# A fused linear-attention and gated-MLP kernel: raw weights ahead of fetches at the turn of the halves, stores of key/value sums spread over rounds, first folded weights in slots of x

## The chip, the cores and the metric

The kernel runs on one core of a Trainium2 chip. The metric is the device time in microseconds (us) from start to end; lower is better. The engines are named as the profile names them: PE (TensorE, matmuls), DVE (VectorE), ACT (ScalarE), POOL (GpSimd) and SP (SyncE, which here issues all transfers). Each engine works through a list of its own in order, and waits where an instruction needs another engine's or a transfer's result.

## The reference

With x of 2048 x 1024, 32 heads of 32 and a hidden width of 3584, all in fp32:

```
xn  = layernorm(x)
q, k, v = split(xn @ wqkv)                       # per head
phi(a) = concat(softmax(a @ w_phi), softmax(-a @ w_phi))
kv  = phi(k)^T @ v ;  z = sum over tokens of phi(k)
s   = ((phi(q) @ kv) / (phi(q) @ z + 1e-6)) @ wo
g   = silu((silu(xn @ w1) * (xn @ w3)) @ w2)
out = x + s * g
```

## The kernel before

**Products.** Each fp32 operand is split into a rounded part and a rest (fp32r), by `split`: ScalarE casts (L91), VectorE subtracts (L92). A product is three passes over these. Blocks of 2 x 2 are multiplied with seven products in place of eight, in the order A11, A12, S2, S1, S3, S4, A22 (`ORDER`), with B-side operands B11, B21, T2, T1, T3, B22, T4; their sums are made by GpSimd (L126, L127, L270, L272) and, for x, by VectorE. TensorE accumulates the seven products in PSUM banks a, b and c.

**Prologue (0 to some 90 us).** x of the first token half is loaded, normalised, transposed and split into the seven operands for four quarters q. The weights of keys and queries are multiplied with w_phi once ("folded"): `first_folds` loads a block `wr`, multiplies it on TensorE (`fold`, L247, three PSUM buffers), lets ScalarE copy it back into `wr` (L311) and SP store it (L312). 22 blocks are folded here, the last nine in three groups of three between the splits of S3, S4 and A22. Their `wr` tiles come from tag "w" of the pool `work`, which has five slots and also holds T2 (`t`), the evicted gate and up results (`h`, `u`) and others. A slot of a fold is free again when its store has landed. The pool `xp` has 14 slots, for blocks of x, and is closed near the end of the first half.

**First stage (to some 1176 us).** Two token halves tb = 0, 1; 28 hidden tiles f each; seven products ("events") of twelve matmuls for each f. From step 7 on the order on all five engines is the program's own, written out by step tables, until the stage ends: `prep_at` says at which step an operand of B is split for (tb, f), normally four events ahead (`LEAD`), `load_at` when the raw weights two tiles on are loaded (`b_load`, L256, L257), one step after the last split of the present tile. Side work has steps of its own; in the second half it is the splitting of w2 and others (`side_w2`, loads `room<-in_w` at L516, sums on GpSimd, splits `w2o`). In the last tile of the first half (f = 27) each event from the first on is followed by the fetch of one operand of x of the second half, four transfers of 512 KB at L162, into the place of the operand just used. The second half begins with its tiles 0 to 6 interleaved in pairs: (0,0), (0,1), (1,0), (0,2), (1,1), and so on, written (f, product).

**Heads (to some 1507 us).** For each of two column halves c and eight pairs of token tiles i, `heads` computes keys and values in seven products, the feature map, and sums phi(k)^T v and z into one PSUM bank `pkv`. The operands of x for the next pair are loaded at the start of a pair (L565). When all pairs of c are summed, `kv_out` copies the sums into `kva` and `zs` and stores them with 16 small transfers (L737, L738), for c = 0 within pair 0 of c = 1, for c = 1 in round 1 of the next stage.

**w2 stage (to some 2040 us).** Rounds r over seven blocks kb and eight pairs of token tiles, with 42 matmuls each (`product`). `a_first` loads `hr` (L769, 512 KB) for the next round, subtracts (`sm`, L774) and splits; `a_second` makes the other operands (L782, L783). `product` evicts with ScalarE (L921) or adds on VectorE (L927); in later blocks ScalarE copies to `u` (tag "h1", two slots) and GpSimd adds. The order is the scheduler's here. Weights arrive by `load_b` (L762). Queries, attention and the output projection end the kernel.

Of the kernel before, what the change touches and what calls it, by code (L numbers as in the profile page):

```python
# [8 lines left out]
F = mybir.dt.float32  # L9
# [7 lines left out]
S, D, H, DH, FF = 2048, 1024, 32, 32, 3584  # L17
P = 128
NT = S // P
ND = D // P  # L20
NF = FF // P
# [7 lines left out]
def tile_kernel(ctx: ExitStack, tc: tile.TileContext, x, wkT, wqT, wv, wphi, wo, w1, w3, w2, out):  # L29
# [106 lines left out]
    work = pool("work", 5)  # L136
# [101 lines left out]
    def load_w(wT, dch, c, t=None):  # L238
        wr = blk("wr") if t is None else t
        nc.sync.dma_start(wr, wT[dch][:, 4 * c:4 * c + 4])  # L240
        return wr
# [37 lines left out]
    for t in range(8):  # L279
        if t in (4, 5):  # L280
            if t == 4:
                late = rwp.tile([P, 2, 2, 512], F, name="rw", tag="rw")
            r = late[:, t - 4]
        else:
            r = quad("xt", F).rearrange("p u k t -> p u (k t)")
        xs.append(load_x(t, [r[:, 0], r[:, 1]]))
        if t == 3:
            rws = [b_load(0)]
            early_w = [load_w(*folds[k][:3], work.tile([P, 4, P], F, name="wr", tag="w")) for k in range(4)]
# [3 lines left out]
    for j in range(4):  # L293
        sl = slice(32 * j, 32 * j + 32)
# [7 lines left out]

    at_fold = 0

    def first_folds(n):
        nonlocal at_fold
        for _ in range(n):
            wT, k, c, d = folds[at_fold]
            wr = early_w.pop(0) if early_w else load_w(wT, k, c, work.tile([P, 4, P], F, name="wr", tag="w"))
            pw = fold(wr, c)  # L310
            nc.scalar.copy(wr, pw)  # L311
            nc.sync.dma_start(d, flat(wr))  # L312
            at_fold += 1
# [42 lines left out]
    for n in ("S3", "S4", "A22"):  # L356
        next(b_gen)
        for q in range(4):
            first_split(n, q, raw[q][n])
        first_folds(3)  # L360


    def load_kv(c, k):
# [33 lines left out]
    for tb in range(2):  # L397
        for f in range(NF):
            own = [at_event[tb, f, j] for j in range(7)]
            steps = [k - LEAD for k in own]  # L400
            if (tb, f) == (1, 1):
                steps = [k - 2 for k in own]
            elif (tb, f) == (1, 2):
                steps = [own[0] + k for k in (-2, -2, -1, 0, 1, 2, 2)]
            if (tb, f) != (0, 0):
                for k in steps:
                    prep_at.setdefault(k, []).append((tb, f))
                sums_at.setdefault(steps[0] - (1 if tb and f in (1, 2) else 2), []).append((tb, f))
            late = divmod(NF * tb + f + 2, NF)
            if late[0] < 2:  # L410
                load_at.setdefault(max(steps[6] + 1, 0) if (tb, f) != (0, 0) else 0, []).append(late)
# [265 lines left out]
                nc.tensor.matmul(pkv[sl, m], e[:, m // 4, (m % 4) * P + 32 * h:(m % 4) * P + 32 * h + 32],  # L677
                                 v[:, 4 * (m % 4) + h], start=first and m == 0, stop=last, skip_group_check=True)

    pkv = None  # L680

    def heads(i, xo, wb, steps, pend):

        nonlocal pkv
        bank, first, last = {}, i == 0, i + 1 == len(pairs)
        for b, an, bn in ORDER:
            if b not in bank:
                bank[b] = ps.tile([P, 512], F, name=f"bank{b}", tag=f"bk{b}", bufs=BANKS[b])
            n = 0
            for k in range(4):  # L690
                for u, w in PASSES:
                    nc.tensor.matmul(bank[b], xo[an][:, u, k], wb[bn][:, w, k], start=an in ("A11", "A12", "S1") and n == 0,  # L692
                                     stop=LAST[b] == an and n == 11, skip_group_check=True)
                    n += 1
            pb, pv = bank[b], bank[b].rearrange("p (h d) -> p h d", d=DH)
            if an == "A11":
                k0 = work.tile([P, 512], F, name="k0", tag="w")
                nc.scalar.copy(k0, pb)
            elif an == "A12":
                nc.vector.tensor_add(k0, pb, k0)  # L700
                e0, v0 = room_ev()
                keys(k0, e0)
            elif an == "S2":
                d0 = value(v0)
                nc.scalar.copy(d0, pv)
            elif an == "S1":
                if pend:
                    kv(*pend)
                    if first:
                        kv_out(0, pkv)  # L710
                e1, v1 = room_ev()
                d1 = value(v1)
                nc.scalar.copy(d1, pv)
            elif an == "S3":
                nc.vector.tensor_add(d1, pv, d1)
            elif an == "S4":
                nc.vector.tensor_add(d0, pv, d0)
            else:
                if first:
                    pkv = ps.tile([P, 512], F, name="pkv", tag="kv", bufs=1)[:, :8 * (DH + 2)]  # L720
                    pkv = pkv.rearrange("p (h d) -> p h d", d=DH + 2)
                kv(pkv, first, False, e0, v0)
                keys(pb, e1)
            next(steps)
        return pkv, False, last, e1, v1

    def kv_out(c, pkv):
        kva = work.tile([P, 8, DH], F, name="kva", tag="w")
        zs = small.tile([P, 8], F, name="zs")
        nc.scalar.copy(kva, pkv[:, :, :DH])  # L730

        nc.vector.tensor_scalar_add(zs[:, :4], pkv[:, :4, DH], 1e-6)
        nc.vector.tensor_copy(zs[:, 4:], pkv[:, 4:, DH])
        for s in range(2):
            for j in range(4):
                sl = slice(32 * j, 32 * j + 32)
                nc.sync.dma_start(kv_d[j % 2, s, :, G * c + j // 2:G * c + G:2], kva[sl, 4 * s:4 * s + 4])  # L737
                nc.sync.dma_start(z_d[0, c, :, j, s].rearrange("g f -> f g"), zs[sl, 4 * s:4 * s + 4])  # L738

# [37 lines left out]
    def a_second(hq, sm, _):  # L779
        hr = hq.rearrange("p b (h k) t -> p b h k t", h=2)  # L780
        s34 = work.tile([P, 4, P], F, name="s34", tag="w")
        nc.vector.tensor_sub(s34[:, 0:2], hr[:, 1, 1], sm)  # L782
        nc.vector.tensor_sub(s34[:, 2:4], hr[:, 0, 1], sm)  # L783
        t1, t2 = quad("as"), quad("as")
        split(t1[:, 0], t1[:, 1], hq[:, 1])
        split(t2[:, 0], t2[:, 1], s34)
        return {"S1": (t1, 0), "A22": (t1, 2), "S3": (t2, 0), "S4": (t2, 2)}
# [146 lines left out]
    for r, new in enumerate(steps):  # L934
        kb, i = new or (NKB, 0)
        end = kb == NKB - 1
        if new is None:
            in_order(ENG.SP, ENG.Activation, ENG.DVE, ENG.Pool)
            xT = split_q(xf)
        if kb + 1 < NKB and 1 < i < 7:  # L940
            load_b(kb + 1, i - 2)
        parts = first
        if r + 1 < len(steps) - 1:
            first = a_first(*steps[r + 1])
        bank = {}
        for b, an, bn in TURN:
            if an in FIRST:
                if new:
                    product(kb, i, bank, r, parts[2], b, an, bn)
            elif old:  # L950
                product(*old, banks, r, second, b, an, bn)
                if new is None:
                    load_wo(2 * BNAMES.index(bn))
                    load_wo(2 * BNAMES.index(bn) + 1)
        if new:
            second = a_second(*parts) if r else ready[1]
        if r == 1:

            kv(*pend)
            kv_out(1, pkv)  # L960
            late_rw += [rwp.tile([P, 2, 2, 512], R, name="late", tag="rw") for _ in range(2)]
        if i + 1 == len(pairs):
            if end:
                for k in range(6):
                    load_wo(k)
            else:
                load_b(kb + 1, 5)
                load_b(kb + 1, 6)


        if end:
            if i:
                gate(*pairs[i - 1])
            if i in (1, 2):
                for k in range(4 * i - 4, 4 * i):
                    load_wq(1, k, ring("wq1"))
            if i == 3:
                zb = [flat(ring("zb").bitcast(F)) for _ in range(2)]
                for c in range(2):
                    nc.sync.dma_start(zb[c], z_d[:, c].rearrange("o g j s f -> o (g j s f)").to_broadcast([P, D]))  # L980
            if 1 < i < 6:
                for j, t in enumerate(pairs[i - 2]):
                    load_wq(0, 2 * i - 4 + j, accp.tile([P, 2, 512], R, name="wq0", tag=f"acc{t}"))
            if i == 4:
                xf = load_q(0)
            elif i == 5:
                xT = split_q(xf)
            elif i > 5:
                if i == 6:

                    kvu = work.tile([P, 2 * G, DH], F, name="kvu", tag="h1", bufs=2)
                    nc.sync.dma_start(kvu, kv_d.rearrange("a s f g d -> (a s f) g d"))
                es[7 - i] = queries(project_q(xT, 7 - i, "bka"), 7 - i)
            if i == 7:
                xf = load_q(1)
        old, banks = new, bank
# [94 lines left out]
```

## Time and profile before

| | |
|---|---|
| runs | 2465.31 us (median of 3; 2465.04 to 2466.66) |
| profiled execution | 2466.53 us, span 2464.8 us |
| TensorE busy | 2406.8 us, 98% of the span |
| mean granted TensorE clock | 0.996 |
| VectorE, ScalarE, GpSimd busy | 71%, 36%, 28% |
| transfers | 521 MB, mean 211 GB/s |

In a row of a timeline the first number is the start in us from the beginning of the span, the second the time of the row's instructions together, then engine, line, operation, what is written and read, the shapes and the count. Behind it, in brackets, stands the idle time of the engine ahead of the row and what ended it. In a list of waits stand the total, the number and the longest. A row of windows gives, for each engine in the order PE, weight loads, DVE, ACT, POOL, the busy time and count, then the granted clock, the share of the DMA engines and GB/s.

### The profile page before, as it was taken

Reading aid. Unit: us, or ns where it says so; the run is one execution under the profiler, and the core shown is the slowest. Engines: PE = TensorE matmul, PEld = TensorE weight load, DVE = VectorE, ACT = ScalarE, POOL = GpSimd, SP = SyncE. Lnnn points to the kernel's source line nnn. Section 1 sums busy time; section 2 is a strip of 40 time slices with the busy share of each in tenths; the row PEclk is TensorE's granted clock in tenths of the full one; section 3 lists DMA queues with packets and bytes.
Section 4 is the critical chain, followed back from the end, with each engine's and each line's share of the span. In section 5 each row is a group of like instructions: output and inputs, shape, how many; then the busy total and the mean of one; then the engine's idle time right before and its main releaser. Section 6 shows DMA issues by size and latency. Waiting matters only on the chain.

```text
span 2464.8 us, 35933 instructions
## 1 busy us (share of the span) xinstructions
PE 2406.8 (98%) x13648; PEld 1971.2 (80%) x13648; DVE 1748.6 (71%) x2573; ACT 887.4 (36%) x1555; POOL 681.8 (28%) x481
## 2 busy tenths in 40 slices
PE   5999999999999999999999999999999999999999
PEld 5788788888788888888788788788888887777877
DVE  8578876664688888764566565687878887777775
ACT  6455544443354454432111113422222244222221
POOL 2334554432455555431000000011111112232222
PEclk9999999999999999999999999999999999999999
DMA  8556999775988887755967763623444376223222
GB/s 296 170 198 228 328 320 303 260 230 175 303 296 293 288 296 278 247 179 199 354 211 297 271 204 123 235 95 138 179 171 180 109 280 232 93 73 92 76 86 69
DMA packets 300812, 521.02 MB, mean 211 GB/s; under 512 B 24544, under 2 KB 172000, under 8 KB 298848
## 3 DMA queue, kind: packets, MB, share of 16 engines
q1 hardware_dynamic: 300640, 518.74, 61.1%
q8 instruction: 107, 1.75, 0.3%
q14 instruction: 65, 0.53, 0.1%
HBM read 331.22 MB, written 187.44 MB: 210 GB/s over the span
## 4 chain that ended last, share of the span: by engine, by line
PE 84%; DVE 6%; DMA 4%; SPq 2%; issue 2%; ACT 1%; POOL 1%; ACTq 0%; DVEq 0%; POOLq 0%
PE bankb L598 19%; PE pm L100 14%; PE bankb L915 12%; PE bankc L598 9%; PE bankb L692 7%; PE bankc L915 6%; PE banka L598 5%; PE bankc L692 3%; PE banka L915 3%; PE banka L692 2%; DVE bo L92 1%; PE po L1019 1%; PE pt L1013 1%; PE pkv L677 1%; DMA xoA<-xo_d0A 1%
## 5 line engine op out<-in xcount | busy, mean ns | idle before, releaser
L92 DVE TENSOR_TENSOR bo<-rw,bo 128x512 fp32r<-128x512 f32 x336 | 289.0, 863 | 214.9 <-ACT bo L91 212.6
L91 ACT CAST bo<-rw 128x512 fp32r<-128x512 f32 x336 | 206.9, 618 | 47.7 <-DMA rw<-in_w 8.8
L915 PE MATMUL bankb<-bo,as 128*128 128x512 f32 x816 | 201.6, 390 | 3.8 <-DVE acc L927 3.8
L925 POOL TENSOR_TENSOR acc<-acc,u 128x512 f32<-128x512 f32 x48 | 63.3, 1319 | 481.0 <-ACT u L924 472.6
L100 PE MATMUL pm<-wq,xh 128*128 128x512 f32 x768 | 185.7, 394 | 0.0
L270 POOL TENSOR_TENSOR rw<-rw,t 128x512 f32<-128x512 f32 x56 | 82.2, 1467 | 370.0 <-DVE bo L92 369.8
L915 PEld LDWEIGHTS bankb<-bo,as 128*128 128x128 f32 x816 | 153.3, 188 | 36.0 <-DVE acc L927 4.2
L598 PE MATMUL bankb<-op1A,bo 128*128 128x512 f32 x672 | 159.7, 393 | 8.9 <-ACT bo L91 4.7
L598 PE MATMUL bankb<-op0A,bo 128*128 128x512 f32 x672 | 160.9, 392 | 7.6 <-ACT bo L91 4.5
L598 PE MATMUL bankb<-op0S,bo 128*128 128x512 f32 x672 | 162.8, 391 | 4.8 <-ACT u L623 4.0
L100 PEld LDWEIGHTS pm<-wq,xh 128*128 128x128 f32 x768 | 141.9, 188 | 31.5 <-issue 3.0
L598 PE MATMUL bankc<-op0S,bo 128*128 128x512 f32 x672 | 163.0, 391 | 0.4 <-DVE op0S L92 0.3
L598 PE MATMUL bankb<-op1S,bo 128*128 128x512 f32 x672 | 161.6, 390 | 0.5 <-ACT u L623 0.5
L598 PE MATMUL bankc<-op1S,bo 128*128 128x512 f32 x672 | 161.2, 389 | 0.0
L598 PEld LDWEIGHTS bankb<-op1A,bo 128*128 128x128 f32 x672 | 126.7, 189 | 37.9 <-DVE u L631 6.0
L598 PEld LDWEIGHTS bankb<-op0A,bo 128*128 128x128 f32 x672 | 125.4, 188 | 34.6 <-ACT bo L91 4.7
L598 PEld LDWEIGHTS bankb<-op0S,bo 128*128 128x128 f32 x672 | 125.4, 188 | 31.7 <-ACT u L623 4.9
L598 PEld LDWEIGHTS bankb<-op1S,bo 128*128 128x128 f32 x672 | 126.0, 188 | 27.4 <-ACT u L623 1.2
L915 PE MATMUL bankc<-bo,as 128*128 128x512 f32 x576 | 147.3, 391 | 0.3 <-DVE as L92 0.3
L598 PEld LDWEIGHTS bankc<-op1S,bo 128*128 128x128 f32 x672 | 126.2, 188 | 26.2
L598 PEld LDWEIGHTS bankc<-op0S,bo 128*128 128x128 f32 x672 | 125.4, 188 | 26.7 <-DVE op0S L92 0.7
L884 POOL TENSOR_TENSOR ez<-e,zb 128x1024 f32<-128x1024 f32 x32 | 76.7, 2395 | 218.0 <-issue 122.9
(210 smaller groups left out, 4792.9 us busy)
## 6 DMA issues: line engine op xcount, KB each, us to landing
rw<-in_w SPq DMA_DIRECT2D x112, 512.0 KB, 4.6
hr<-h_d SPq DMA_DIRECT2D x56, 512.0 KB, 3.7
h_d<-h SPq DMA_DIRECT2D x111, 256.0 KB, 4.0
xoS<-xo_d0S SPq DMA_DIRECT2D x32, 512.0 KB, 8.7
xoS<-xo_d1S SPq DMA_DIRECT2D x32, 512.0 KB, 3.6
room<-in_w SPq DMA_DIRECT2D x56, 256.0 KB, 7.0
xoA<-xo_d0A SPq DMA_DIRECT2D x24, 512.0 KB, 9.6
xoA<-xo_d1A SPq DMA_DIRECT2D x24, 512.0 KB, 3.6
```

The lines of the kernel that those rows point to most:

```text
L91: nc.scalar.copy(hi, src)
L92: (by or nc.vector).tensor_sub(lo, src, hi.bitcast(F))
L100: nc.tensor.matmul(p, xT[dch][:, a], w(dch, b), start=n == 0, stop=n == 3 * ND - 1)
L270: nc.gpsimd.tensor_sub(b11, b22, t2)
L598: nc.tensor.matmul(bank[b], bos[tb, f][bn][:, w, k], ao[an][:, u, k], start=first and n == 0, stop=LAST[b] == an and n == 11, skip_group_c ...
L677: nc.tensor.matmul(pkv[sl, m], e[:, m // 4, (m % 4) * P + 32 * h:(m % 4) * P + 32 * h + 32], v[:, 4 * (m % 4) + h], start=first and m == 0 ...
L692: nc.tensor.matmul(bank[b], xo[an][:, u, k], wb[bn][:, w, k], start=an in ("A11", "A12", "S1") and n == 0, stop=LAST[b] == an and n == 11, ...
L884: nc.gpsimd.tensor_mul(ez, ef, zb[c])
L915: nc.tensor.matmul(bank[b], t[:, u, pos + k], bos[kb, bn, k][:, w], start=first and n == 0, stop=LAST[b] == an and n == 5, skip_group_chec ...
L925: nc.gpsimd.tensor_add(c, c, u)
L1013: nc.tensor.transpose(pt[:, g, :], e[:, (4 * q + g) * P:(4 * q + g + 1) * P], ident)
L1019: nc.tensor.matmul(po[32 * g:32 * g + 32, hh, q * P:(q + 1) * P], kvu[sl, G * c + 4 * q + g], et[sl, g], start=True, stop=True, skip_group ...
```

## The change

Four things change.

1. `first_folds` takes a maker of tiles. For the last nine folds it is None, and `load_w` then takes a block of the pool `xp` in place of tag "w".
2. In the last tile of the first half the step of the seventh split, and with it the load of the raw weights of tile 1 of the second half, is one smaller. On SP these two loads then stand ahead of the fetch of operand S3, where they stood behind it.
3. `kv_out` stores nothing itself and returns four closures of four stores each (j = 3 first when popped). One is called after each of the first four products of the next pair, i = 1 (sums of c = 0), and one in each round from r = 2 on (c = 1).
4. `kva` is of tag "h1" with two slots in place of tag "w".

In the built program the lists of the engines differ as follows. In the prologue all lists are alike up to the thirteenth fold. Behind its eviction ScalarE's list now has: the cast of T2 of tile 1, the S1 cast of the last quarter, the table load and Silu of the first `h`, the S2 and S4 casts, then the evictions of the nine folds with casts of tile 1 between them; `h` itself is copied earlier. TensorE's list has four S1 products, the nine folds among the remaining S1, S2 and S3 products, then S4 and A22 of tile 0, and only then eleven of A11's and all of A12's matmuls of tile 1. In the c = 0 heads part the 16 stores still stand close together, but behind the loads of the next pair and one load of weights. In the w2 stage four of them stand ahead of each of the next `hr` loads.

```diff
-    def first_folds(n):
+    def first_folds(n, t=lambda: work.tile([P, 4, P], F, name="wr", tag="w")):
...
-            wr = early_w.pop(0) if early_w else load_w(wT, k, c, work.tile([P, 4, P], F, name="wr", tag="w"))
+            wr = early_w.pop(0) if early_w else load_w(wT, k, c, t and t())
...
             first_split(n, q, raw[q][n])
-        first_folds(3)
+        first_folds(3, None)
...
             steps = [k - LEAD for k in own]
-            if (tb, f) == (1, 1):
+            if (tb, f) == (0, NF - 1):
+
+                steps[6] -= 1
+            elif (tb, f) == (1, 1):
...
-    pkv = None
+    pkv, out_now = None, []
...
                     if first:
-                        kv_out(0, pkv)
+                        out_now.extend(kv_out(0, pkv))
...
             next(steps)
+            if out_now and not first:
+                out_now.pop()()
         return pkv, False, last, e1, v1
...
-        kva = work.tile([P, 8, DH], F, name="kva", tag="w")
+        kva = work.tile([P, 8, DH], F, name="kva", tag="h1", bufs=2)
...
-        for s in range(2):
-            for j in range(4):
-                sl = slice(32 * j, 32 * j + 32)
+
+        def store(j):
+            sl = slice(32 * j, 32 * j + 32)
+            for s in range(2):
                 nc.sync.dma_start(kv_d[...], kva[...])
                 nc.sync.dma_start(z_d[...], zs[...])
+
+        return [lambda j=j: store(j) for j in range(4)]
...
+        if out_now and r:
+            out_now.pop()()
         if r == 1:
             kv(*pend)
-            kv_out(1, pkv)
+            out_now += kv_out(1, pkv)
```

## The prediction

> **What bounds the kernel now.** I read the page's busy shares first, then TensorE's waits by releaser, then the timelines of the three places that the edits touch.
>
> ```profile
> PE 2406.8 (98%) x13648; PEld 1971.2 (80%) x13648; DVE 1748.6 (71%) x2573; ACT 887.4 (36%) x1555; POOL 681.8 (28%) x481
> PE pt L215 <- DVE xt L210: 15.3, 2, 12.7
> PE bankb L598 <- ACT bo L91: 9.2, 2, 4.7
> PE bankb L915 <- DVE acc L927: 3.8, 1, 3.8
> ```
>
> TensorE works 2406.8 of 2464.8 us; the edits can only touch the other 58, and 15.3 of these wait for x at the start. The waits (total, times, longest) hold two single stalls that the edits face: 4.7 us of `ACT bo` at the turn of the halves, 3.8 us of `DVE acc` behind the c=1 stores. The slots of edit 1 concern the prologue, where TensorE also waits in small pieces.
>
> **Edit 1, nine folds in slots of x (prologue).** TensorE before, then ScalarE, GpSimd:
>
> ```profile
> 56.53 3.92 PE L247 MATMUL pw<-bd,wr 128*128 128x128 f32 x32
> 73.75 1.65 PE L598 MATMUL bankb<-op0S,bo 128*128 128x512 f32 x6 [0.79 <-ACT h L618]
> 81.17 3.02 PE L598 MATMUL bankb<-op0S,bo 128*128 128x512 f32 x12 [1.01 <-ACT u L623]
> 84.02 2.88 PE L598 MATMUL bankc<-op0S,bo 128*128 128x512 f32 x12
> 86.74 2.88 PE L598 MATMUL bankb<-op0A,bo 128*128 128x512 f32 x12
> 91.27 1.07 PE L598 MATMUL bankb<-op0S,bo 128*128 128x512 f32 x4
> ...
> 60.97 1.31 ACT L91 CAST op0S<-xf 128x512 fp32r<-128x512 f32 x2
> 73.12 0.58 ACT L618 COPY h<-bankb 128x512 f32<-128x512 f32 x1 [1.33 <-DMA wq_d<-wr]
> 75.24 0.62 ACT L91 CAST bo<-t 128x512 fp32r<-128x512 f32 x1 [1.54 <-POOL t L127]
> 77.22 1.28 ACT L621 ACT_TABLE_LOAD   x1
> 78.52 0.63 ACT L621 ACTIVATE h<-h 128x512 f32<-128x512 f32 x1
> ...
> 56.71 6.06 POOL L126 TENSOR_TENSOR rw<-rw 128x512 f32<-128x512 f32 x1 [26.45 <-DMA rw<-in_w]
> 73.91 1.29 POOL L127 TENSOR_TENSOR t<-rw 128x512 f32<-128x512 f32 x1 [11.14 <-DMA wq_d<-wr]
> ```
>
> Before, the folds hold the five "w" slots until their stores land: `t` (T2 of f=1) waits 11.14 us for one, `h` 1.33 us. TensorE's small waits (0.79, 1.01) come of that. Freeing the slots looks like a gain.
>
> But the scheduler orders ScalarE anew. In the changed program the cast of T2 stands right after the eviction of the thirteenth fold, the last in the old slots, and behind it, in order, stand the S1 cast of the last x quarter, the table load and activation, the S2 and S4 casts and all later fold evictions. Before, these casts ran at 60.97, long before T2's at 75.24. T2 needs GpSimd: L126 ends at 56.71+6.06 = 62.77 (nothing in the edit makes it start earlier, its raw weights have the same place), L127 ends 1.29 later at 64.1, the cast 0.62 later at 64.7, the S1 cast at 65.3. TensorE's list is the same up to the second fold of the row at 56.53, which ends at 56.53 + 3.92/2 = 58.5; next stand the S1 products. So TensorE stands from 58.5 to 65.3, 6.7 us.
>
> Common end: f=1's S2, at 91.27 before. From 58.5 both programs do the same work up to it: nine folds at 3.92/4 = 0.98 to 1.02, and 83 matmuls (60 of f=0, 23 of f=1) at (86.74−84.02)/12 = 0.227: 28.0 us of 32.8. So 4.8 us of the old stretch is lost time, replaced by 6.7 of idle: +1.9. (Were nothing put in its place, −4.8: the good end.) The clock after such an idle is read from the turn, quoted next: after 4.68 us idle a group took 4.86 instead of 2.88 us, +2.0. Sum **+3.9**. The later fold evictions run behind the table load, but three banks and the half clock on TensorE hide that: no charge. Nothing pays it back, because no deadline follows: the half runs at its own pace for 500 us. Ends: −4.8 to +8.7 (the rivals).
>
> One rule of the Trainium skill weighs on this list: "ScalarE: Activation LUTs", What ACT_TABLE_LOAD costs, gives a load about 1.28 us and then a drain of about 1.38. Here the row at 77.22 took 1.28, and the activation began 0.02 us later, so this trace shows no drain; by the page the S2 and fold steps would come 1.38 us later, and an estimate of the sum would be about +5.3 in place of +3.9.
>
> **Edit 2, raw weights one place earlier (turn).**
>
> ```profile
> 633.54 4.86 PE L598 MATMUL bankb<-op1A,bo 128*128 128x512 f32 x12 [4.68 <-ACT bo L91]
> 657.29 2.88 PE L598 MATMUL bankb<-op1S,bo 128*128 128x512 f32 x12
> 662.74 2.43 PE L598 MATMUL bankc<-op1S,bo 128*128 128x512 f32 x10
> 686.13 5.73 PE L598 MATMUL bankb<-op1A,bo 128*128 128x512 f32 x24 [0.72 <-DVE u L631]
> ...
> 619.88 6.23 SPq L162 DMA_DIRECT2D op1S<-xo_d1S  x4
> 626.21 1.34 SPq L256 DMA_DIRECT2D rw<-in_w  x1
> 642.29 2.86 SPq L516 DMA_DIRECT2D room<-in_w  x4
> 632.87 0.62 ACT L91 CAST bo<-rw 128x512 fp32r<-128x512 f32 x1 [8.81 <-DMA rw<-in_w]
> 649.13 0.62 ACT L91 CAST w2o<-room 128x512 fp32r<-128x512 f32 x1 [1.41 <-DMA room<-in_w]
> 653.70 1.18 DVE L92 TENSOR_TENSOR bo<-rw,bo 128x512 fp32r<-128x512 f32 x1
> 659.91 1.78 DVE L92 TENSOR_TENSOR bo<-rw,bo 128x512 fp32r<-128x512 f32 x1
> 632.00:635.00 3.00, 1.36 (x3) 0.82 (x4) 1.17 (x2) 1.62 (x3) 0.90 (x1) 0.79 1.05 340
> ```
>
> The raw weights leave at 626.21 behind the S3 fetch and are cast at 632.87, 6.7 later. Put before that fetch they leave at about 619.9 and are cast at 626.6, so the event that could begin at 633.54 − 4.68 = 628.9 does not wait: 4.68 + 1.98 = 6.7 us vanish there. The S3 fetch slips by two issues, some 2.9 us: its last part leaves at 626.1 + 2.9 and lands 6.7 later, at about 635.7; five more events of 2.72 stand between 628.9 and its own, at about 642, which cover it.
>
> What is late next: the `room` loads. The DMA share is 1.05 and 340 GB/s in the window row: saturated, and the same bytes stand ahead of these loads, so they still arrive at 649. VectorE's list is fixed in this stretch: the bo of the tenth event of this half stands behind the w2o work and ends at 653.70+1.18 = 654.9, where TensorE came at 657.29 (2.4 to spare); the next at 659.91+1.78 = 661.7 against 662.74 (1.05 to spare). So of 6.7 at most 1.05 survives 662.7, and at 686.13 TensorE waits for VectorE anyway. I take **−0.5**; ends −6.7 and 0.
>
> **Edits 3 and 4, stores in four rounds, their tile in tag h1.** For c=0:
>
> ```profile
> 1354.90 0.32 SPq L737 DMA_DIRECT2D kv_d<-kva  x1
> 1369.86 0.85 SPq L565 DMA_DIRECT2D xoA<-xo_d0A  x2
> 1358.50 0.76 PE L677 MATMUL pkv<-ev 128*32 128x34 f32 x64 [0.88 <-DVE ev L717]
> ```
>
> SP spends 15 us on 16 stores, then loads x for the next pair; TensorE's only stall nearby is for `ev`, which the stores do not touch. **0**; the cover is the lead of the loads, which are needed one pair later. For c=1:
>
> ```profile
> 1523.04 0.32 SPq L737 DMA_DIRECT2D kv_d<-kva  x1
> 1534.42 0.38 SPq L769 DMA_DIRECT2D hr<-h_d  x1
> 1541.57 0.53 SPq L769 DMA_DIRECT2D hr<-h_d  x1
> 1543.18 0.42 DVE L774 TENSOR_TENSOR sm<-hr 128x256 f32<-128x256 f32 x1 [10.02 <-DMA hr<-h_d]
> 1544.26 2.23 PE L915 MATMUL bankb<-bo,as 128*128 128x512 f32 x6 [3.81 <-DVE acc L927]
> 1547.67 1.59 PE L915 MATMUL bankc<-bo,as 128*128 128x512 f32 x4 [0.33 <-DVE as L92]
> 1532.13 1.52 PE L915 MATMUL bankc<-bo,as 128*128 128x512 f32 x6
> 1557.28 1.52 PE L915 MATMUL bankc<-bo,as 128*128 128x512 f32 x6
> ```
>
> The `hr` load stands on SP behind all 16 stores (1523.04 to 1534.42), lands 8.8 us after issue, and VectorE, in order, holds `sm` and behind it the `acc` eviction that TensorE's bank needs. The two rows of the same product in rounds r=3 and r=5 are 25.15 us apart; two undisturbed rounds of seven products of six matmuls are 2 × 42 × 0.227 = 19.06, so 6.1 us is lost. With four stores ahead of it, at (1534.42 − 1523.04)/16 = 0.71 each, `hr` leaves at about 1525.9 and lands by 1534.7. It feeds the group after the one that could begin at 1544.26 − 3.81 = 1540.4, that is at about 1541.8, and its casts took 4.5 us (1543.18 to 1547.67), so it is needed by 1537.3: 2.6 us to spare. The second `hr`, behind four more stores and the weights, leaves about 8 us earlier than 1541.57 and is needed a round later. The stall goes: **−6.1**; ends −6.1 and 0. The tile's new tag: its two slots are otherwise used tens of us later, 0.
>
> **Sum.** +3.9 − 0.5 + 0 − 6.1 = −2.7 against the profiled execution's 2466.5, so 2463.8; that execution lies 1.2 above the median 2465.31, so the forecast is 2462.6 us, a tenth of a per cent. About 0.2%, 4.9 us, is what a measurement here tells from no change.
>
> **Rivals.**
> The prologue doesn't stall. For: `t` waits 11.14 us for its slot before, and 4.8 us are lost there. Against: the in-order list of ScalarE. With 0 to −4.8 the total is −6.6 to −11.4: 2453.9 to 2458.7, likelier the upper half.
>
> The turn pays in full: VectorE's work between 650 and 690 drains earlier, as its inputs from raw weights come earlier. For: several of its operations take 1.78 where 1.18 or less is seen, so there is slack to win. Against: `room` at 649.13. Total 3.9−6.7−6.1 = −8.9: 2456.4.
>
> Other side, GpSimd is starved in the prologue: L126 took 6.06 where L127 took 1.29, while VectorE ran without a pause. If VectorE still runs during L127 in the new order, T2 comes 4.8 later and TensorE idles 11.5: edit 1 costs +8.7, the total is +2.1, 2467.4; and the S1, S2 and S4 casts, the table load and the activation queued behind T2 (3 × 0.62 + 1.28 + 0.63 = 3.8 us) then hold the fold evictions too, up to another 3.8: 2471.2. It decides from 6.6 for edit 1 upward, that is when the S1 products start after 68. The Trainium skill's "GPSIMD Engine Reference", Key points, says that GpSimd shares its SBUF interfaces with VectorE and contends with instructions of two SBUF inputs; the 6.06 agrees.
>
> `hr` still late: the first `hr` takes over 11.4 us (1525.9 to 1537.3) so the c=1 stall stays: total +3.4, 2468.7, more if later rounds wait for their four stores too. Against: 8.8 us from issue to landing even among 2 MB of weights. This is also the case that the spreading does nothing.
>
> **How the numbers follow.** Forecast 0.45 (its own range 2460 to 2465.5; 0.05 of it under the bound of faster, 0.40 within), prologue without stall 0.14 (faster), turn in full 0.14 (0.12 faster, 0.02 same), GpSimd starved 0.17 (0.07 same, 0.10 slower), `hr` late 0.10 (half same, half slower). Faster 0.31, same 0.54, slower 0.15. Range 2455.5 to 2469.5: it takes in both faster rivals and the centres of the slower ones, and leaves out the best end of the first and the tails of the last two.
>
> **What would show it.** Right: TensorE idle of 6 to 7 us near 58 to 65 waiting for ScalarE or S1, with lower clock after it, and f=1's S2 near 95; no wait at 628 to 634, but waits on VectorE near events ten and twelve of the second half; no `acc` stall, and rounds 9.52 us apart from r=1 on. Wrong: S1 products at 61, the lead of 6.7 us after the turn still there at 700, or a wait for `hr` in any round.

## The result and the profile after

The changed kernel takes 2475.81 us (median of 7 runs, 2471.32 to 2476.30) against 2466.66 us for the kernel before in the same series (7 runs, 2465.04 to 2469.02): ratio 1.0031 [1.0021, 1.0041], taken over all runs, slower by 0.2 to 0.4%. The forecast was 2462.6 us, no measurable change, and the range ended at 2469.5.

The profiled execution took 2473.01 us, so the two traces lie 6.5 us apart, less than the medians (9.2). Its page and TensorE's list of waits (total, times, longest):

```profile
span 2471.2 us, 35930 instructions
PE 2405.3 (97%) x13648; PEld 1970.4 (80%) x13648; DVE 1743.0 (71%) x2573; ACT 886.6 (36%) x1555; POOL 678.3 (27%) x481
```

```profile
PE bankb L923 <- ACT acc L929: 7.3, 1, 7.3
PE bankc L601 <- ACT op0S L91: 5.2, 1, 5.2
PE bankc L601 <- DVE bo L92: 2.4, 1, 2.4
PE bankb L923 <- DVE acc L935: 1.4, 1, 1.4
PE pkv L680 <- issue: 0.5, 1, 0.5
```

TensorE does the same work, 2405.3 us, so what changed are its waits. The 4.7 us of `ACT bo` at the turn is gone. The 3.8 us behind the c=1 stores, which should have gone too, is now 7.3 and 1.4. The 5.2 is the prologue stall that was forecast, and "issue" is a wait that the kernel before did not have.

To see where the span's 6.4 us came from, I compare the start of the same work in both timelines. Rows of before that were not shown yet, then those of after:

```profile
52.52 0.80 PE L598 MATMUL bankb<-op0A,bo 128*128 128x512 f32 x1 [4.49 <-ACT bo L91]
163.69 3.06 PE L598 MATMUL bankb<-op0A,bo 128*128 128x512 f32 x12 [1.20 <-DVE u L631]
1521.78 0.77 PE L677 MATMUL pkv<-ev 128*32 128x34 f32 x64
2066.63 0.94 PE L1019 MATMUL po<-et,kvu 64*32 64x128 f32 x32
```

```profile
51.07 0.80 PE L601 MATMUL bankb<-op0A,bo 128*128 128x512 f32 x1 [4.50 <-ACT bo L91]
164.66 3.04 PE L601 MATMUL bankb<-op0A,bo 128*128 128x512 f32 x12 [1.22 <-DVE u L634]
686.48 5.73 PE L601 MATMUL bankb<-op1A,bo 128*128 128x512 f32 x24 [0.71 <-DVE u L634]
1523.25 0.77 PE L680 MATMUL pkv<-ev 128*32 128x34 f32 x64
2072.83 0.94 PE L1029 MATMUL po<-et,kvu 64*32 64x128 f32 x32
```

| from | to | before | after | difference | predicted |
|---|---|---|---|---|---|
| start | first product A11 | 52.52 | 51.07 | −1.5 | 0 |
| A11 | 164 (edit 1) | 111.2 | 113.6 | +2.4 | +3.9 |
| 164 | 686 (edit 2) | 522.4 | 521.8 | −0.6 | −0.5 |
| 686 | last sum of keys and values (c=0 stores) | 835.7 | 836.8 | +1.1 | 0 |
| last sum | first `po` (c=1 stores) | 544.85 | 549.58 | +4.7 | −6.1 |
| first `po` | end of the span | 398.2 | 398.4 | +0.2 | 0 |

How far chance moves these stretches is read from the kernels of the experiments below that leave a stretch as it was: A11 began at 51.2 to 53.0; the second row took 110.2 to 112.0, the third 522.4 to 525.7 (in kernels with neither edit 1 nor edit 2), the fourth 834.2 to 836.9 (in all kernels but the four with the change's own c=0 stores), the fifth 543.3 to 546.1. Only the second row and the fifth stand clear of that. So −0.6 and +1.1 can't be told from nothing by this table, and neither can −1.5, which lies ahead of any difference between the programs.

The last stretch but one is the miss: 10.8 us between what was forecast and what came. SyncE, VectorE and TensorE of after in that stretch:

```profile
1526.29 0.39 SPq L777 DMA_DIRECT2D hr<-h_d  x1
1534.79 0.32 SPq L777 DMA_DIRECT2D hr<-h_d  x1
1542.15 0.32 SPq L743 DMA_DIRECT2D kv_d<-kva  x1
```

```profile
1542.16 0.43 DVE L782 TENSOR_TENSOR sm<-hr 128x256 f32<-128x256 f32 x1 [10.39 <-DMA hr<-h_d]
1551.17 0.42 DVE L782 TENSOR_TENSOR sm<-hr 128x256 f32<-128x256 f32 x1 [3.61 <-DMA hr<-h_d]
```

```profile
1543.83 2.93 PE L923 MATMUL bankb<-bo,as 128*128 128x512 f32 x6 [7.35 <-ACT acc L929]
1546.56 1.77 PE L923 MATMUL banka<-bo,af 128*128 128x512 f32 x6
1562.03 1.65 PE L923 MATMUL bankb<-bo,as 128*128 128x512 f32 x6 [1.44 <-DVE acc L935]
```

The first `hr` did leave at 1526.29, behind four stores, as predicted (1525.9). But it landed 15.8 us later, at 1542.1, and not 8.8. The second, 16.4 us after issue, was late again.

The list of ScalarE had changed too. Before, then after:

```profile
1535.05 0.59 ACT L921 COPY acc<-bankb 128x512 f32<-128x512 f32 x1 [0.77 <-PE bankb L915]
1543.18 0.62 ACT L91 CAST af<-hr 128x512 fp32r<-128x512 f32 x1 [7.55 <-DMA hr<-h_d]
```

```profile
1542.16 0.62 ACT L91 CAST af<-hr 128x512 fp32r<-128x512 f32 x1 [14.02 <-DMA hr<-h_d]
1543.20 0.58 ACT L929 COPY acc<-bankb 128x512 f32<-128x512 f32 x1
```

Before, four evictions (1530.97 to 1535.05) stood ahead of the casts of `hr`. In after they stand behind the first of these casts, so TensorE waits for a bank (`ACT acc`), four groups of six matmuls earlier in its list than before.

### The profile page after: what moved, and what is told of

It reads as the page before. It is cut to its first block, busy times and chain, and to the rows that moved or that the text cites. A ratio compares the mean times of both kernels' runs of the same rounds, so it can differ in the third digit from the quotient of the medians.

```text
span 2471.2 us, 35930 instructions
## 1 busy us (share of the span) xinstructions
PE 2405.3 (97%) x13648; PEld 1970.4 (80%) x13648; DVE 1743.0 (71%) x2573; ACT 886.6 (36%) x1555; POOL 678.3 (27%) x481
## 4 chain that ended last, share of the span: by engine, by line
PE 88%; DVE 5%; DMA 3%; ACT 1%; issue 1%; POOL 0%; SPq 0%; ACTq 0%; DVEq 0%; POOLq 0%
PE bankb L601 22%; PE pm L100 14%; PE bankb L923 12%; PE bankc L601 10%; PE bankb L695 7%; PE bankc L923 6%; PE banka L601 5%; PE bankc L695 3%; PE banka L923 3%; PE banka L695 2%; DVE bo L92 1%; PE po L1029 1%; DMA hr<-h_d 1%; PE pkv L680 1%; PE pt L1023 1%
```

## The experiments

Ratios are to the kernel before on the same chip, with a 95% interval. "Stage" is the stretch from the last sum to the first `po`: 544.85 us before, 549.58 after.

**Each edit alone.** First the nine folds in slots of x, and nothing else:

```diff
-        first_folds(3)
+        first_folds(3, None)
```

> Edit 1 alone. In the changed kernel TensorE stood 5.2 us before the S1 products and reached the same product 1.0 us later than before (2.4 later if the start of the prologue, which ran 1.4 ahead, is chance). Theory: edit 1 costs 1 to 2.5 us, the idle of about 5 us stands at the S1 products, and the rest of the kernel is as before. Rival (the prologue's cost is chance): 0.

Measured 2470.88 us (11 runs) against 2468.33 (21 runs): 1.0015 [1.0006, 1.0023], slower by 0.06 to 0.23%, some 1.5 to 5.7 us. The stretch from A11 to the wait at 164 took 114.7 us; in the kernels without this edit it took 110.2 to 112.0, mean 111.2. TensorE, then ScalarE of this run:

```profile
62.43 0.80 PE L598 MATMUL bankc<-op0S,bo 128*128 128x512 f32 x2 [4.49 <-ACT op0S L91]
```

```profile
59.40 0.62 ACT L91 CAST bo<-t 128x512 fp32r<-128x512 f32 x1 [0.57 <-POOL t L127]
61.76 0.62 ACT L91 CAST op0S<-xf 128x512 fp32r<-128x512 f32 x1 [1.74 <-DVE xf L232]
```

The stall is there, but here T2 is early (59.40) and the S1 cast waits for VectorE. In after it was the other way round:

```profile
61.18 0.62 ACT L91 CAST bo<-t 128x512 fp32r<-128x512 f32 x1 [3.14 <-POOL t L127]
61.70 0.61 ACT L91 CAST op0S<-xf 128x512 fp32r<-128x512 f32 x1
62.37 2.08 PE L601 MATMUL bankc<-op0S,bo 128*128 128x512 f32 x4 [5.19 <-ACT op0S L91]
```

Counted from A11, the S1 cast begins 8.5 us in before (60.97 − 52.52), 10.6 in after and 10.2 here. So some 2 of the 5 us come of a later S1, held by T2 in the one run and by VectorE in the other. The rest comes of TensorE's order: S1's products now stand ahead of the folds that filled this time before.

What the stretch lost is not seen any more at 686: from A11 to there the traced execution took 636.1 us, where the kernels with neither edit 1 nor edit 2 took 633.6 to 636.3. It was the fastest of the eleven, and the runs together are slower, so the traces leave open how much of the loss is paid back.

The raw weights one place earlier, alone:

```diff
+            if (tb, f) == (0, NF - 1):
+                steps[6] -= 1
```

> Edit 2 alone. Theory: the 4.7 us wait of the third event of the second half is gone, TensorE waits instead for bo of VectorE near the tenth and twelfth events, and at 686 us the gain is about 0.6 us: -0.6. Rival (the gain is paid in full when the prologue is left alone): -6.7.

Measured 2469.24 us (11 runs): 1.0005 [0.9996, 1.0014], no difference. In the profile the wait at the turn goes and comes back later: here twice within the event that the prediction calls the tenth (counted from 0), in after at its tenth and twelfth. TensorE of this run, then of after:

```profile
656.29 0.50 PE L601 MATMUL bankb<-op1S,bo 128*128 128x512 f32 x1 [4.27 <-ACT bo L91]
659.34 4.81 PE L601 MATMUL bankb<-op1S,bo 128*128 128x512 f32 x11 [2.54 <-DVE bo L92]
```

```profile
653.85 2.79 PE L601 MATMUL bankb<-op1S,bo 128*128 128x512 f32 x11 [1.23 <-DVE bo L92]
661.99 4.26 PE L601 MATMUL bankc<-op1S,bo 128*128 128x512 f32 x11 [2.40 <-DVE bo L92]
```

In this run, whose trace is of its slowest execution, the first cast of `room` came at 653.58, against 649.13 before and 648.02 in after, and the two waits alone, 6.8 us, are as long as the wait at the turn and its slow group had been in before (6.7).

The stores alone (edits 3 and 4, as in the change):

```diff
-                        kv_out(0, pkv)
+                        out_now.extend(kv_out(0, pkv))
...
+        if out_now and r:
+            out_now.pop()()
```

> Edits 3 and 4 alone. Theory of bursts: each group of small stores holds back the packets of the loads behind it by 6 to 9 us, so four groups in four rounds cost more than one group of sixteen: +4 to +6 us, in rounds r=3 to r=6 of the w2 stage. Rival (the loss comes of the three edits together, through another order in the prologue or the turn): 0 or the -6.1 that was forecast.

Measured 2477.82 us (5 runs): 1.0044 [1.0030, 1.0057], slower by 0.3 to 0.6%. This edit alone costs as much as the whole change. Stage 554.45, worse than in after. TensorE at c=0 and c=1:

```profile
1398.42 0.27 PE L677 MATMUL pkv<-ev 128*32 128x34 f32 x4 [1.84 <-issue]
1547.25 2.93 PE L920 MATMUL bankb<-bo,as 128*128 128x512 f32 x6 [8.07 <-ACT acc L926]
1568.00 2.93 PE L920 MATMUL bankb<-bo,as 128*128 128x512 f32 x6 [3.21 <-DVE acc L932]
```

**Is it the number of stores ahead of `hr`?** If a queue of stores delays `hr`, letting almost none go ahead of it should help. c=1's 16 stores in one go in round 3; `hr` then stands behind three of them:

```diff
-        if out_now and r:
-            out_now.pop()()
+        if r == 3:
+            while out_now:
+                out_now.pop()()
```

> As edits 3 and 4 alone, but the sixteen stores of c=1 at once in round 3, so that on SP the first hr load stands ahead of thirteen of them. Theory of bursts: one group only, the first hr lands in about 5 us and the c=1 stall of before (6.1 us) shrinks to 0 to 2 us at the next hr load: -4 to -6. Rival (what costs is the spread over rounds on ScalarE's and VectorE's lists, not the transfers): as stores_alone, +5. Rival (only the number of stores counts): 0.

Measured 2478.48 us (5 runs): 1.0049 [1.0036, 1.0061], stage 551.25. The expectation was wrong. VectorE, then TensorE:

```profile
1539.67 0.42 DVE L779 TENSOR_TENSOR sm<-hr 128x256 f32<-128x256 f32 x1 [5.72 <-DMA hr<-h_d]
1559.88 0.42 DVE L779 TENSOR_TENSOR sm<-hr 128x256 f32<-128x256 f32 x1 [13.12 <-DMA hr<-h_d]
```

```profile
1541.65 1.65 PE L920 MATMUL bankb<-bo,as 128*128 128x512 f32 x6 [1.63 <-ACT acc L926]
1563.10 2.93 PE L920 MATMUL bankc<-bo,as 128*128 128x512 f32 x6 [8.91 <-ACT acc L926]
```

With only three stores ahead of it `hr` (issued at 1529.32) still took 10.3 us, and the next (issued at 1544.93, behind the other thirteen) took 14.9. So counting the issue time of the stores ahead, as the prediction did, doesn't give the landing. The other thirteen stand right behind the first `hr`, so this run does not tell stores ahead from stores beside. What remained was the packets. From the records of single transfers, packets of 4096 bytes (all loads here) that began in each microsecond, number and mean duration:

```
          before           after            z in rows, spread (below)
1527      -                11 x 5.73 us     18 x 0.16 us
1531      -                 8 x 1.89        98 x 0.16
1536       3 x 4.69        59 x 0.18        94 x 0.16
1538       9 x 1.95        56 x 0.56       103 x 0.16
1541      49 x 0.22        23 x 0.40        -
1544     100 x 0.16        63 x 0.18        -
1549     102 x 0.16         6 x 1.52        48 x 0.16
```

In before and after, load packets behind a group of stores take up to 4.7 and 8.6 us in place of 0.16, and the loads crawl for 6 to 9 us. Before, that happened once (1536 to 1541). In after it happened behind each of the four groups.

**Which stores?** `kv_out` has two kinds: keys x values in packets of 128 bytes, z in packets of 4 bytes. One kind spread over the rounds, the other stored at once, and the reverse:

```diff
-        return [lambda j=j: store(j) for j in range(4)]
+        for j in range(4):
+            zst(j)
+        return [lambda j=j: kvs(j) for j in range(4)]
```

> As edits 3 and 4 alone, but the eight z stores (packets of 4 bytes) go at once and only the eight kv stores (128 bytes) are spread over the four rounds. Theory of bursts, the 4-byte packets being the cause: the stalls in rounds r=4 to 6 go, one stall of some 6 us stays: about as before, 0 to +2. If the 128-byte packets are the cause: as stores_alone, +6 to +10 by the stage.

> The reverse: the eight kv stores at once, the eight z stores spread. 4-byte packets the cause: as stores_alone, +5 to +10. 128-byte packets the cause: 0 to +2. If both kinds do it, both kernels of this pair are slower by 5 or more.

Against 2467.26 us of before (24 runs). Sums spread, z at once: 2467.40 us (10 runs), 0.9999 [0.9990, 1.0008]. z spread, sums at once: 2479.11 (4 runs), 1.0043 [1.0027, 1.0058]. Stages 545.74 and 555.50. The transfers issued from 1515 to 1562, with KB each and median us to landing, of the second:

```profile
hr<-h_d SPq DMA_DIRECT2D x4, 512.0 KB, 13.7
kv_d<-kva SPq DMA_DIRECT2D x8, 16.0 KB, 1.5
z_d<-zs SPq DMA_DIRECT2D x8, 0.5 KB, 15.1
```

The eight stores of 128-byte packets, 1024 packets, land in 1.5 us. Behind the first two z stores (256 packets of 4 bytes) eleven load packets took 6.5 us in the mean. In the other run, with the sums spread, 128-byte packets ran among the loads from 1543 to 1548, and the load packets took 0.16 us. It is the z stores.

**Another queue.** The c=1 stores on ScalarE's queue, so that no load stands behind them in one queue:

```diff
-                nc.sync.dma_start(z_d[...], zs[...])
+                (nc.scalar if c else nc.sync).dma_start(z_d[...], zs[...])
```

> Edits 3 and 4 alone, but the sixteen stores of c=1 are issued by ScalarE on its own DMA queue. If the loads are held up because they stand behind the stores in one queue, the stall of c=1 is gone: -4 to -6 against before. If the DMA engines themselves are held up by small stores of any queue, the packets of hr are slow as in stores_alone and it costs +5 or so.

Measured 2477.34 us (7 runs): 1.0037 [1.0027, 1.0048]. Load packets were slow here too (1535 to 1548), so what is held up is not one queue. And ScalarE now stands behind its own stores:

```profile
1539.21 0.59 ACT L926 COPY acc<-bankb 128x512 f32<-128x512 f32 x1 [9.34 <-DMA kv_d<-kva]
```

**No 4-byte packets.** First, one store for each tile as it lies (packets of 1 KB and 32 bytes), with the rearranging moved to where the sums are read, by ScalarE copies (`wide`) or GpSimd copies (`wide2`):

```diff
-        for s in range(2):
-            for j in range(4):
...
+        nc.sync.dma_start(kv_d[c], kva)
+        nc.sync.dma_start(z_d[c], zs)
```

> The kernel before, with none of the four edits, but the sums are stored as they lie: one store of 1 KB rows for kv and one of 32 bytes per partition for z, for each c, and rearranged when they are read back (sixteen loads of 128-byte pieces, and ScalarE copies of z). Theory of small stores: no burst of 16, so hr lands in time and the c=1 stall of 6.1 us is gone: -5 to -6.5. Rival (hr is late for another reason, the weights loaded around it): 0.

> As wide (sums stored as they lie), but the copies that rearrange z on reading are made by GpSimd in place of ScalarE. In wide the stall of c=1 was gone, but four waits at the end of the w2 stage and in the attention took 5 us. If these come of the copies on ScalarE: -4 to -6 against before. If they come of the sixteen loads of 128-byte pieces: about 0, as wide.

`wide`: 2466.55 us (11 runs), 0.9996 [0.9988, 1.0005]; `wide2`: 2468.69 (10 runs), 1.0001 [0.9992, 1.0011]. In `wide`, `hr` landed in 3.3 us (median of five; the first two in 6.7 and 8.3) and TensorE had no wait between 1521 and 1570. But the stage took 542.73 and 543.49, 1 to 2 us less than before and not 6, since waits came up at its end, where the sums are read, and behind it (first `po` to the end: 402.4 and 399.6 us, 398.1 before). TensorE of `wide`:

```profile
2011.77 1.19 PE L912 MATMUL bankc<-bo,as 128*128 128x512 f32 x4 [1.71 <-DVE as L92]
2056.09 1.66 PE L912 MATMUL bankc<-late,as 128*128 128x512 f32 x6 [1.51 <-DVE acc L924]
2097.34 1.17 PE L1027 MATMUL po<-et,kvu 64*32 64x128 f32 x32 [2.48 <-ACT et L1023]
```

They stay when GpSimd copies (1.78, 1.41, 0.83), so ScalarE's copies alone are not their cause. Which of the moved loads and copies is, stays open.

Second, z turned by TensorE into eight rows before it is stored, two stores with packets of 128 bytes, nothing else changed from the kernel before (the z stores are now two in place of eight); then the same with the spreading of edits 3 and 4, and with edit 2:

```diff
-                nc.sync.dma_start(z_d[0, c, :, j, s].rearrange("g f -> f g"), zs[sl, 4 * s:4 * s + 4])
+        nc.tensor.transpose(zt[0], zs, ident)
+        zw = small.tile([8, P], F, name="zw")
+        nc.scalar.copy(zw, zt[0])
+        for s in range(2):
+            nc.sync.dma_start(z_d[0, c, :, :, s], zw[4 * s:4 * s + 4].rearrange("g (j f) -> g j f", f=DH))
```

> The kernel before, with none of the four edits; zs is turned on TensorE (one 128 x 8 transpose into the free end of the bank of pkv, evicted by ScalarE) and z is stored in two stores with packets of 128 bytes in place of eight with packets of 4 bytes. If the 4-byte packets alone hold up the loads: the c=1 stall of 6.1 us is gone, -4 to -6 by the stage. If any small packet does: the stall stays, 0.

> Edits 3 and 4 alone with the same two z stores of 128-byte packets, in the rounds r=2 and r=3. If the prediction's step (stores ahead of hr on SP cost only their issue, and hr lands in time) was right but for the 4-byte packets: the stage is 4 to 6 us shorter than before, some 10 us shorter than with edits 3 and 4 alone. If spreading itself costs, through the lists of ScalarE and VectorE: slower than before by 4 or more.

> zrows with edit 2: a candidate for the best of all. -4 to -7 against before; edit 2 itself is worth 0 to -0.6.

| | us (runs) | ratio | stage |
|---|---|---|---|
| z in rows | 2462.25 (10) | 0.9976 [0.9967, 0.9986] | 538.83 |
| z in rows, spread | 2461.40 (11) | 0.9977 [0.9968, 0.9986] | 538.89 |
| z in rows, edit 2 | 2460.94 (10) | 0.9974 [0.9965, 0.9983] | 538.87 |

All three are faster than before (2468.57 us, 31 runs), by 0.14 to 0.35%; they can't be told from each other. The same window of after and of z in rows, spread (busy us and count of PE, weight loads, DVE, ACT, POOL; granted clock, DMA share, GB/s):

```profile
1530.00:1535.00 5.00, 5.00 (x24) 4.14 (x23) 1.10 (x2) 0.00 (x0) 0.00 (x0) 1.00 0.57 31
```

```profile
1530.00:1535.00 5.00, 5.00 (x24) 4.14 (x23) 3.23 (x7) 2.63 (x5) 0.00 (x0) 1.00 1.01 353
```

31 GB/s at a DMA share of 0.57 is what held-up packets look like here: the engines are counted as busy and move almost nothing. With rows of 128 bytes the same loads run at 353 GB/s. The transfers issued from 1515 to 1562 of after, then of z in rows, spread:

```profile
hr<-h_d SPq DMA_DIRECT2D x4, 512.0 KB, 16.1
```

```profile
hr<-h_d SPq DMA_DIRECT2D x5, 512.0 KB, 3.5
```

Once the packets are mended, spreading the stores adds nothing to the stage (538.83 and 538.89): `hr` behind all ten stores is early enough. The spread kernel also has `kva` in tag "h1" (edit 4) and is no slower, so edit 4 costs nothing that shows.

## Why the prediction was wrong

**Edit 1, predicted +3.9, about +3 up to 164.** Right in kind, and near in size: +2.4 in after and +3.5 alone, by the mean of the unedited kernels. The idle was 5.2 and 4.5 us, not 6.7. In after T2 was ready earlier: L126 on GpSimd took 2.97 us, not the 6.06 of the trace of before. Alone L126 took 1.41, and VectorE held the S1 cast. So the row of 6.06 was a bad duration to carry over. What sets it is open: alone VectorE ran beside GpSimd without a pause, as before, but its three subtractions from 56.48 took 4.04 us, where after has 1.90 for three; so the two engines may share the loss in either way, which no run here tests. The clock loss came, but was half of the forecast: four products took 2.08 us behind the idle, where four at full clock take 1.07 (the row at 91.27 of before), at a granted clock of 0.50; the 48 folds behind them took 6.18 us, as fast each as before (4.07 for 32). The step "S1 stands behind the cast of T2" held in after only; alone, VectorE took its place with the same outcome. "Nothing pays it back" is not shown, as said above. The rival without a stall and the one with GpSimd starved both did not come.

**Edit 2, predicted −0.5, measured −0.6.** Right in the way named, and the number is luck. The stall at the turn goes, and VectorE's fixed list is met at the tenth and twelfth events, with waits of 1.23 and 2.40 us. But from the first product of the second half to 686 the kernels without this edit took 61.8 to 65.3 us (mean 63.3), and the three with it 61.5 (after), 62.0 (z in rows, edit 2) and 65.8 (alone). No gain and no loss is shown.

**The c=0 stores, predicted 0, measured +1.1, alone +3.1.** Probably wrong, by a term I had not looked for: +1.1 lies within what this stretch varies by, +3.1 (838.8 us) does not. The prediction looked at the wait for `ev` alone, "which the stores do not touch". Instructions, too, arrive as packets on the DMA engines. The wait is "issue": it is there in all four kernels whose c=0 stores are those of the change (0.5, 1.8, 2.0 and 2.1 us in total), and in no other. In three of them (the stores alone, c=1 in one go, c=1 on ScalarE's queue) a packet of instructions, 16 KB, took 3.6, 3.7 and 3.3 us right behind the c=0 stores, where 0.95 is seen in before. Each had landed some 2.3 us before TensorE's wait began (1394.2 and 1396.6 with the stores alone), and in after no slow packet was caught. The same happens in before behind the c=1 stores (3.65 us at 1527.55), and there no wait follows. So the slow packet is shown, and that it makes the wait is argued. About 0.7 of its 1.1 us lie at this wait (the `pkv` products begin 0.56 later than in before, what follows them 1.3); the rest is spread thin.

**The c=1 stores, predicted −6.1, measured +4.7.** The step that failed is "`hr` leaves at about 1525.9, lands 8.8 us after issue, and lands by 1534.7". The issue was right to 0.4 us. The 8.8 us was taken as what 512 KB need in that place, and it was itself the tail of the stores: in before `hr` leaves just behind them, and with no 4-byte stores ahead the first `hr` landed in 3.8 us (z in rows, spread) and 5.3 (z in rows). So spreading does not take `hr` out from behind the stores, it puts a hold-up ahead of every `hr`, and makes each longer: 15.8 and 16.4 us. Against z in rows the stage of after is 10.7 us longer, and the rows shown add up to it: 7.35 + 1.44 idle, and (2.93 − 1.52) + (1.77 − 1.52) + (1.65 − 1.52) of slow matmuls, 10.6.

"It is needed by 1537.3: 2.6 us to spare" failed as well, though it cost little beside the first. TensorE stood from 1536.48 (1543.83 − 7.35) and went on 1.7 us after the landing, so `hr` was needed by 1534.8, 8.5 us after issue and not 11.4. `late_once` gives 8.7 (10.3 us to landing, 1.63 of wait). The reason is ScalarE's new list, with the casts of `hr` ahead of four evictions, where the prediction had counted from the list of before. With a landing of 8.8 us this would have cost some 0.3.

The rival that came is "`hr` still late", at a chance of 0.10. Its threshold of 11.4 us was too long by this, and its price too low: it stopped at "the stall stays", total +3.4 or 2468.7, and named "more if later rounds wait" without a number. What I had set against it, 8.8 us "even among 2 MB of weights", was the same mistaken row. A look at the single packets of that row, 4.69 us for 4 KB at 1536 and 0.16 at 1544, would have told it from a full queue. So would this window of before, 26 GB/s at a DMA share of 0.63:

```profile
1535.00:1540.00 5.00, 5.00 (x24) 4.14 (x23) 0.00 (x0) 0.59 (x1) 0.00 (x0) 1.00 0.63 26
```

The −6.1 itself was the right prize: z in rows takes 6.0 us off the stage, by another way than the one predicted.

## What to carry to other kernels

A landing time read in a trace belongs to what ran ahead of it: before moving a load or a store, look at the duration of single packets around it, and at GB/s beside the DMA share. Where small-packet stores hold up loads, mend the packets (here one TensorE transpose and a copy, 0.2%) before the schedule; spreading them here put a hold-up ahead of each load. An edit that hardly moves its own resource can still cost elsewhere by reordering an engine's list, as the folds did, and as the casts of `hr` on ScalarE did: read a deadline from the list of the new program. And before a difference of a us is put down to an edit, see how far the same stretch moves in kernels that leave it alone.

## What was not expected of the hardware

Stores in packets of 4 bytes take 7 to 9 ns each in the records and look free. Loads issued behind them pay: 256 such packets, and the next eleven 4 KB packets took 6.5 us in the mean in place of 0.16. It was seen across queues (the stores on ScalarE's) and for packets of instructions (3.65 us in place of some 0.95). 128-byte packets, a thousand of them, and 128 of 32 bytes did nothing of the kind. Nor do all 4-byte packets: 16 more come with each transfer (416 beside the 2048 of the 16 stores in before, for 26 transfers from 1515 to 1562), and with 15 of them to the us the load packets took 0.16 us (before, at 1547). The Trainium skill, "DMA: Bandwidth & Descriptors", Specifications, names 512 bytes as the least size for full rate, with a read-modify-write below it. The direction agrees, but the stores' own rate was not what hurt, and at 128 and 32 bytes no harm was seen. Whether the size of the stores' packets or their strided places in memory does it, and why loads pay, stays open: no run separates them.

A pause of 2.40 us was enough to slow TensorE: eleven products behind it took 4.26 us in place of some 2.5 (eleven at 0.227), at a granted clock of 0.62 in the window below, while behind the 1.23 us pause the clock stayed at 1.00.

```profile
662.00:666.00 4.00, 4.00 (x11) 3.18 (x12) 3.54 (x6) 0.03 (x1) 0.92 (x1) 0.62 0.45 154
653.80:656.40 2.60, 2.55 (x11) 2.13 (x12) 0.78 (x1) 1.16 (x3) 2.52 (x3) 1.00 0.96 299
```

The Trainium skill, "TensorE: Matmul & The Clock Gate", Part 1, has the clock halve after an idle window of about 3.4 us. The 5.19 and 7.35 us idles here agree; the 2.40 us one is shorter than that, so here the measurement decides. In the trace's clock records of after, every stretch but the one cut off at the end is a multiple of 3.41 us; the halved one here runs from 662.96 to 666.37, and in the 3.41 us before it TensorE worked 1.01 us.
